# Windowed attention with sinks and a gated feed-forward block on one core: an early gate unit, scores in threes, and groups 2 and 3 turned by the crossbar

## The chip, the cores and the metric

The kernel runs on one core of a Trainium2 chip. The metric is device time in microseconds for one launch. The engines named here are TensorE (PE, with PEld for its weight loads), VectorE (DVE), ScalarE (ACT), GpSimd (POOL) and SyncE (SP). POOL and SP, and in places ACT, also issue the transfers (DMAs), which all run on the same sixteen DMA engines.

## What is computed

Attention over 4 batches, 8 heads, 768 positions and head size 64, in which a query sees the last 128 positions and the first 4 ("sinks"), followed by a gated feed-forward block on all 3072 tokens:

```python
keep = is_sink | in_window            # pos < 4, or 0 <= q - k < 128
a = softmax(where(keep, q @ k.T / 8, -1e9))
x = (a @ v) as [3072 tokens, 512]
g = x @ w_gate                        # 512 x 1536
out = (g * sigmoid(g) * (x @ w_val)) @ w_out   # 1536 x 512
```

## The kernel before, in words

Tokens are handled in twelve groups of 256, three to a batch. Heads go in four pairs. For a group the attention steps are:

- **Loads.** POOL loads keys and queries (`natp`, four buffers) and values, with a cast to bf16. `load4` puts four tokens of each head in a row (two DMAs, for groups below `NPE = 4`); `load1` puts one token with all its heads in a row (four DMAs, for the others). `load_gate` and `load_out` load the feed-forward weights in chunks. POOL's queue is in order, and each of its loads waits for the load issued eight before it.
- **Turning keys and queries.** Scores need them with the head size on the partitions. For groups 0 to 3 TensorE does it (`step_T`: 64 small matmuls into PSUM, then copies by ACT and DVE). For groups 4 to 11 the crossbar does it (`cross_T`: two transposing DMAs on SP's queue, for the two halves of 128 tokens). `C(g)` is `cross_T(g)` and then the load of group g+4.
- **Scores.** `step_S(g, p2)` computes two head pairs into four PSUM banks; ACT takes exponentials, DVE multiplies by the mask. `step_K(g)` does the scores against the four sinks for all heads, `step_ks` first collects their keys, and `build_vsb` builds on POOL the table of sink values.
- **Values.** `step_PV(g, j, hh)` multiplies by the values for one half of the tokens and four heads; DVE (and for half of group 1 ACT) normalises into `xn`.
- **Turning the output.** For groups below `NXPE = 5` by TensorE (`step_X`), for others by a transposing DMA on SP's queue.

The feed-forward block works on eight blocks of tokens (`SIZES`: three of 256, four of 512, one of 256); block 3 is groups 3 and 4. A `gate` unit projects 512 columns twice (`pg` for the gate, `pv` for the value), with a tanh on ACT between and two DVE operations that make `ht`; `down` multiplies 128 tokens of `ht` by `w_out` and stores the result by SP.

The order is written out by hand. `weave` walks through a list of units (gates, then downs, of one or more blocks), and runs the attention steps of each unit's slot in the middle of it: in a gate between `pg` and `pv`, in a down spread over its twelve matmuls. DVE operations of attention steps are put in the list `later` and issued after the gate's own product, by `flush`. PSUM has eight banks, given out in turn to every product.

At the start TensorE does groups 0 and 1 with little feed-forward work to mix in. Line numbers below are those of the profile.

Of the kernel before, what the change touches and what calls it, by code (L numbers as in the profile page):

```python
# [8 lines left out]
FP32 = mybir.dt.float32  # L9
# [6 lines left out]
def kernel(  # L16
# [12 lines left out]
    nc = tc.nc  # L29
# [13 lines left out]
    SIZES = [256, 256, 256, 512, 512, 512, 512, 256]  # L43
    assert sum(SIZES) == NTOK and NG == 12 and S == 768
    OFF = [sum(SIZES[:i]) for i in range(len(SIZES))]
    NPE = 4
    NXPE = 5
    VS = 72
    FCH = [2, 2, 2, 2, 4]
    assert sum(FCH) == DFC  # L50
# [4 lines left out]
    def pool(name, bufs, psum=False):  # L55
        if psum:
            return ctx.enter_context(
                tc.tile_pool(name=name, bufs=bufs, space=bass.MemoryType.PSUM))
        return ctx.enter_context(tc.tile_pool(name=name, bufs=bufs))
# [2 lines left out]
    wpool = pool("wpool", 1)  # L62
    natp = pool("natp", 4)
    vpool = pool("vpool", 1)
    kqtp = pool("kqtp", 3)
    crossp = pool("crossp", 4)
    epool = pool("epool", 2)
    espool = pool("espool", 2)
# [11 lines left out]
    def bank(shape, dtype, name):  # L80
        return psum.tile(shape, dtype, tag="b", name=name)
# [121 lines left out]
    for ks in kss:  # L203
# [8 lines left out]
        out=dh, in_=dh, compare_op=ALU.is_ge, fill=0.0, base=NS - 1,  # L212
        pattern=[[32, NP2], [NS, 2]], channel_multiplier=-1)
    load_v(1)
    build_vsb(0)
    for i in range(1, 5):
        load_gate(i)

    def build_masks():

# [87 lines left out]
    def step_ks(b):  # L308

        dst = kss[b].rearrange("q (a m) -> q a m", m=KS)  # L310
        for h in range(2):
# [2 lines left out]
                out=dst[r, :, h * NS:(h + 1) * NS],  # L314
                in_=kTs[b * GC][r, :, 0:NS] if b * GC < NPE
                else cross[b * GC][r, 0, 0, :, 0:NS])
    def step_S(g, p2):

        b, c = divmod(g, GC)
        if p2 == 0:  # L320
            e_t[g] = epool.tile([P, H, 512], BF16, tag="e", name="e")

        parts = [(2 * c, 0, 2, P), (2 * c + 1, 1, 1, 3 * P)]
        if c > 0:
            parts.insert(0, (2 * c - 1, 0, 1, 0))
        lo = 0 if c > 0 else P
        pss = [bank([P, 512], FP32, "s") for _ in range(4)]
        for pp in range(2):
            p = 2 * p2 + pp
            for t, j, n, col in parts:  # L330
                for h in range(2):
                    r = slice(h * D, (h + 1) * D)
                    nc.tensor.matmul(  # L333
                        pss[2 * pp + h][:, col:col + n * P], keys(b, t, r, p),
                        queries(g, r, p, j, n), start=True, stop=True)
        m = (mask if c > 0 else mask0).rearrange("q (o a) x -> q o (a x)", o=1)
        for pp in range(2):
            h0 = 4 * p2 + 2 * pp
            for h in range(2):
                nc.scalar.activation(  # L340
                    e_t[g][:, h0 + h, lo:512], pss[2 * pp + h][:, lo:512],
                    AF.Exp, scale=scale)

            def dve(e=e_t[g][:, h0:h0 + 2, lo:512]):
                nc.vector.tensor_tensor(  # L345
                    e, e, m[:, :, lo:512].broadcast_to([P, 2, 512 - lo]), op=ALU.mult)
            later.append(dve)

    def step_K(g):
        b, c = divmod(g, GC)  # L350
        if c == 0:
            return
        ps = bank([P, 256], FP32, "pk")
        for p in range(NP2):

            nc.tensor.matmul(
                ps[KS * p:KS * (p + 1)], kss[b][:, p * KS:(p + 1) * KS],
                queries(g, slice(0, P), p, 0, 2), start=True, stop=True)
        es_t[g] = espool.tile([P, 256], BF16, tag="es", name="es")
        nc.scalar.activation(es_t[g], ps, AF.Exp, scale=scale)  # L360

    def step_PV(g, j, hh, act=False):
        b, c = divmod(g, GC)
# [61 lines left out]

    hts = {}

    def gate(tb, f, attn):

        n = SIZES[tb]  # L430
        two = 512 // n
        if tb not in hts:
            t = hpool.tile([P, DFC * 512], BF16, tag="ht", name="ht")
            hts[tb] = dense(t, DFC, n)
            if tb == 0:
                hts[1] = t[:, DFC * n:2 * DFC * n].rearrange("p (c n) -> p c n", c=DFC)
        x = xTs[tb]

        def project(ws, name):
            ps = bank([P, 512], FP32, name)  # L440
            for i in range(two):
                fi, fo = FOF[f + i]
                for c in range(DMC):
                    nc.tensor.matmul(  # L444
                        ps[:, i * n:(i + 1) * n], ws[fi][:, c, fo * P:(fo + 1) * P],
                        x[:, 0:n // P, c], start=(c == 0), stop=(c == DMC - 1))
            return ps

        pg = project(wgs, "pg")
        th = tpool.tile([P, 512], FP32, tag="th", name="th")  # L450
        nc.scalar.activation(th, pg, AF.Tanh, scale=0.5)  # L451
        for a in attn:
            a()
        pv = project(wvs, "pv")

        u = upool.tile([P, 512], BF16, tag="u", name="u")
        nc.vector.scalar_tensor_tensor(u, th, 1.0, pg, op0=ALU.add, op1=ALU.mult)  # L457
        nc.vector.tensor_tensor(  # L458
            hts[tb][:, f:f + two].rearrange("p a n -> p (a n)"), u, pv, op=ALU.mult)
        flush()  # L460

    def last_down(tb, ts):

# [57 lines left out]
        return [A(step_T, g, 0), last]  # L521

    def Ss(g):
        return [A(step_S, g, p2) for p2 in range(2)]

    def PVs(g):

# [4 lines left out]

    def K(g):
        return A(step_K, g)

    def weave(us, slots):
        assert all(i < len(us) for i in slots)
# [31 lines left out]
    first_T(0)  # L569
    build_masks()  # L570
    first_T(1)
    step_S(0, 0)
    warm(1)
    step_S(0, 1)
    warm(2)
    pro(*[lambda: None] * 3)
    step_PV(0, 0, 0)
# [8 lines left out]
    step_T(1, 1, q_late=True)  # L586
    flush()
    step_ks(0)
    step_S(1, 0)
    load4(2)  # L590
    load_v(2)
    for i in range(4):
        load_out(i)
# [2 lines left out]
    for g in (3, 4):  # L596
# [2 lines left out]


    g0, g1, g2 = gates(0), gates(1), gates(2)
    us = [g0[0], (alone, 0, 0), *g0[1:3], *g1[0:3], g0[3], *g1[3:6], *g0[4:6],
          *downs(0), *g2, *downs(1), *downs(2)]
    p1 = [A(step_PV, 1, j, hh, j == 1) for hh in range(2) for j in range(2)]
    weave(us, slots(
        (0, [flush, A(step_S, 1, 1), K(1), A(next_load, 1)]), (1, p1[:2]), (2, p1[2:] + [flush]),
        (3, [A(step_X, 1, 0), A(step_X, 1, 1, True), flush]),
        (9, T(2)), ((10, 11), Ss(2)), (11, [K(2)]),
        (12, PVs(2)[:2] + [flush]), (13, PVs(2)[2:] + [flush]), (13, C(4)),
        (14, [A(step_X, 2, 0), A(step_X, 2, 1, True), flush]),  # L610
        (15, T(3)), ((16, 17), Ss(3)), (17, sinks(1)), ((18, 18, 19, 19), PVs(3)),
        (18, C(5)), ((20, 21), Ss(4)), (21, Xs(3) + [K(4)]),
        ((22, 22, 23, 23), PVs(4)), (24, Xs(4))))

    def pair(ga, gb, sh=0):
        s = sh
        return [((s, s + 2), Ss(ga)), (s + 2, [K(ga)]),
                ((s + 4, s + 5, s + 6, s + 7), PVs(ga)),
                ((s + 6, s + 8), Ss(gb)), (s + 8, [K(gb)]),
                ((11, 11, 12, 12) if s else (10, 11, 12, 13), PVs(gb))]  # L620

    weave(gates(3) + downs(3), slots(
        *pair(5, 6, 2), (2, C(6)), (10, C(7))))
    weave(gates(4) + downs(4), slots((0, sinks(2)), *pair(7, 8), (3, C(8)), (10, C(9)), (14, C(10))))
    weave(gates(5) + downs(5), slots((0, sinks(3)), *pair(9, 10), (10, C(11))))
    weave(gates(6) + gates(7) + downs(6) + downs(7), slots(
        ((0, 2), Ss(11)), (2, [K(11)]), ((4, 5, 6, 7), PVs(11))))


# [33 lines left out]
```

## Time and profile before

| | |
|---|---|
| median of 13 runs | 246.49 us (245.25 to 247.63) |
| the profiled execution: time, span | 247.39 us, 245.7 us |
| TensorE busy, instructions | 235.3 us (96%), 2081 |
| VectorE, ScalarE, GpSimd busy | 65%, 45%, 29% |
| transfers on POOL's queue (q0) | 68832 packets, 13.90 MB |
| transfers on SP's and ACT's queue (q1) | 28416 packets, 12.49 MB |
| pg and pv of all gates (L444) | 74.7 and 74.9 us busy |
| down (L490) | 63.8 us busy |

The span runs from the first instruction to the last; the device time is 1.7 us longer. In the slices of the page each digit is a busy share in tenths of one fortieth of the span (6.14 us). A row of PE's timeline gives start, duration, line, operation and, in brackets, the idle time ahead of it and who ended it. Rows of DMA queues give packets, megabytes as they land, and the time of the packets as a share of sixteen engines; since several packets can be under way at once, the share passes 100%.

### The profile page before, as it was taken

What the parts mean: (1) busy time and instruction counts of PE and PEld (TensorE: products, weight loads), DVE (VectorE), ACT (ScalarE), POOL (GpSimd) and SP (SyncE); (2) the same over time, 40 slices, a digit from 0 to 9 for tenths busy, and PEclk for the clock granted to TensorE, in tenths of its full rate; (3) what the DMA queues carried; (4) which work ended last, traced back from release to release, by engine and by line L of the source; (5) the groups of instructions that cost most, each with busy time, mean ns of one, the idle gap of its engine ahead of it and who ended that gap; (6) DMA issues with size and microseconds to landing.
All of it is one profiled execution on the core that took longest, in us unless ns stands there. A gap on an engine that the chain in (4) does not pass through costs nothing.

```text
span 245.7 us, 5202 instructions
## 1 busy us (share of the span) xinstructions
PE 235.3 (96%) x2081; PEld 136.8 (56%) x2081; DVE 160.4 (65%) x338; ACT 111.8 (45%) x221; POOL 71.2 (29%) x92
## 2 busy tenths in 40 slices
PE   7796999999999999999999999999999999999994
PEld 2475888757855445554445454445454445488443
DVE  2786688937994388891398980398980389877100
ACT  2657436627481365442665612656512662232111
POOL 8796395784279505307100000000000000000000
PEclk9978899999999999999999999999999999999999
DMA  7999999999999995959960244900334200200132
GB/s 138 169 169 179 204 190 204 164 148 172 162 154 175 204 176 53 113 106 110 236 98 1 48 82 129 173 0 1 64 67 131 85 0 3 43 0 3 48 123 87
DMA packets 97704, 27.11 MB, mean 110 GB/s; under 512 B 83728, under 2 KB 94736, under 8 KB 97680
## 3 DMA queue, kind: packets, MB, share of 16 engines
q0 software_dynamic: 68832, 13.90, 67.6%
q1 hardware_dynamic: 28416, 12.49, 24.0%
q10 hardware_dynamic: 432, 0.39, 0.5%
q8 instruction: 16, 0.26, 0.4%
q14 instruction: 8, 0.07, 0.1%
HBM read 28.34 MB, written 6.29 MB: 141 GB/s over the span
## 4 chain that ended last, share of the span: by engine, by line
PE 83%; ACT 6%; DVE 5%; DMA 3%; issue 2%; POOL 0%; DVEq 0%; POOLq 0%; ACTq 0%
PE pd L490 24%; PE pv L444 24%; PE pg L444 22%; PE o L380 6%; ACT e L340 4%; PE s L333 3%; PE pt L269 2%; DMA kq<-in_k_dram 2%; DVE ht L458 1%; DVE u L457 1%; DVE e L345 1%; PE px L416 1%; ACT th L451 1%; DMA out_dram<-ot 1%; DVE xn L392 1%
## 5 line engine op out<-in xcount | busy, mean ns | idle before, releaser
L444 PE MATMUL pv<-xT,wv 128*128 128x256 bf16 (+1 forms) x384 | 74.9, 328 | 1.1 <-DVE ht L458 1.1
L444 PE MATMUL pg<-xT,wg 128*128 128x256 bf16 (+1 forms) x384 | 74.7, 327 | 0.0
L451 ACT ACTIVATE th<-pg 128x512 f32<-128x512 f32 x72 | 43.5, 604 | 61.3 <-PE pg L444 60.8
L457 DVE SCALAR_TENSOR_TENSOR u<-th,pg 128x512 bf16<-128x512 f32 x72 | 49.2, 683 | 30.2 <-ACT th L451 29.7
L490 PE MATMUL pd<-wo,ht 128*128 128x512 bf16 x276 | 63.8, 379 | 0.0
L458 DVE TENSOR_TENSOR ht<-u,pv 128x512 bf16<-128x512 bf16 x72 | 49.5, 688 | 10.7 <-PE pv L444 3.3
L444 PEld LDWEIGHTS <-wg 128*128 128x128 bf16 x384 | 37.5, 98 | 25.5 <-issue 0.2
L444 PEld LDWEIGHTS <-wv 128*128 128x128 bf16 x384 | 34.8, 98 | 21.4 <-issue 3.1
L340 ACT ACTIVATE e<-s 128x512 bf16<-128x512 f32 (+1 forms) x96 | 46.1, 580 | 0.4 <-PE s L333 0.3
L490 PEld LDWEIGHTS <-ht 128*128 128x128 bf16 x276 | 25.7, 97 | 27.6 <-issue 0.2
L494 ACT ACTIVATE ot<-pd 128x512 f32<-128x512 f32 x23 | 13.7, 597 | 53.8 <-PE pd L490 53.8
L345 DVE TENSOR_TENSOR e<-e,mask 128x1024 bf16<-128x1024 bf16 (+1 forms) x48 | 28.9, 641 | 1.4 <-ACT e L340 1.3
L123 POOL DMA_DIRECT2D va<-in_v_dram x24 | 21.3, 892 | 6.3 <-DMA kq<-in_k_dram 3.4
L107 POOL DMA_DIRECT2D kq<-in_k_dram x16 | 14.2, 885 | 26.5 <-DMA kqT<-kq 23.1
L380 PEld LDWEIGHTS <-e 128*128 128x128 bf16 x352 | 17.1, 100 | 7.4 <-DVE e L345 2.1
L392 DVE TENSOR_TENSOR xn<-o,rcp 128x256 bf16<-128x256 f32 x46 | 19.5, 424 | 1.6
L380 PE MATMUL o<-va,e 128*128 128x65 bf16 x352 | 18.8, 197 | 1.4 <-DVE e L345 1.4
L107 POOL DMA_DIRECT2D kq<-in_q_dram x16 | 14.2, 885 | 6.0 <-DMA va<-in_v_dram 2.5
L385 DVE RECIPROCAL rcp<-o 128x4 f32<-128x4 f32 x48 | 8.5, 177 | 10.1 <-PE o L380 10.1
L380 PE MATMUL o<-vsb,es 128*128 128x260 bf16 x32 | 9.1, 283 | 2.5 <-ACT es L360 2.5
L274 DVE CAST qT<-pt 128x512 bf16<-128x512 f32 x7 | 4.6, 687 | 8.5 <-PE pt L269 8.5
L475 DVE TENSOR_SCALAR ot<-pd 128x256 f32<-128x256 f32 x1 | 0.4, 424 | 14.4 <-DMA out_dram<-ot 14.4
(61 smaller groups left out, 109.7 us busy)
## 6 DMA issues: line engine op xcount, KB each, us to landing
out_dram<-ot SPq DMA_DIRECT2D x23, 256.0 KB
va<-in_v_dram POOLq DMA_DIRECT2D x24, 128.0 KB, 7.4
kq<-in_k_dram POOLq DMA_DIRECT2D x18, 128.0 KB, 7.2
kq<-in_q_dram POOLq DMA_DIRECT2D x16, 128.0 KB, 7.6
wo<-in_moe_w_out_dram POOLq DMA_DIRECT2D x4, 384.0 KB, 12.7
wg<-in_moe_w_gate_dram POOLq DMA_DIRECT2D x4, 256.0 KB, 6.8
wv<-in_moe_w_val_dram POOLq DMA_DIRECT2D x4, 256.0 KB, 7.4
kq<-in_k_dram POOLq DMA_DIRECT2D x3, 256.0 KB, 9.9
```

What stands on the lines that cost most here:

```text
L107: nc.gpsimd.dma_start(x[:, j, i].rearrange("p (h d) -> p h d", d=D), src[b, :, t0:t0 + P].rearrange("h m d -> m h d"))
L123: nc.gpsimd.dma_start(va[:, j, :, 0:D], v[b, :, t0:t0 + P].rearrange("h m d -> m h d"))
L340: nc.scalar.activation(e_t[g][:, h0 + h, lo:512], pss[2 * pp + h][:, lo:512], AF.Exp, scale=scale)
L345: nc.vector.tensor_tensor(e, e, m[:, :, lo:512].broadcast_to([P, 2, 512 - lo]), op=ALU.mult)
L380: nc.tensor.matmul(o, l, r, start=(i == 0), stop=(i == len(mms) - 1), skip_group_check=True)
L392: nc.vector.tensor_tensor(xns[g, j][:, 256 * hh:256 * (hh + 1)].rearrange("p (h d) -> p h d", h=4), po[:, :, 0:D], rcp.broadcast_to([P, 4, ...
L444: nc.tensor.matmul(ps[:, i * n:(i + 1) * n], ws[fi][:, c, fo * P:(fo + 1) * P], x[:, 0:n // P, c], start=(c == 0), stop=(c == DMC - 1))
L451: nc.scalar.activation(th, pg, AF.Tanh, scale=0.5)
L457: nc.vector.scalar_tensor_tensor(u, th, 1.0, pg, op0=ALU.add, op1=ALU.mult)
L458: nc.vector.tensor_tensor(hts[tb][:, f:f + two].rearrange("p a n -> p (a n)"), u, pv, op=ALU.mult)
L490: nc.tensor.matmul(po, hts[tb][:, f, ts * P:(ts + 1) * P], wos[f // n][:, f % n], start=(f == 0), stop=(f == DFC - 1))
L494: nc.scalar.activation(ot, po, AF.Copy, scale=0.5)
```

## The change

What the new version does:

- `NPE` falls from 4 to 2 and `NXPE` from 5 to 3: groups 2 and 3 are loaded by `load1` and turned by `cross_T` on SP's queue, and the outputs of groups 3 and 4 are turned by transposing DMAs. The steps `T(2)`, `T(3)`, `Xs(3)`, `Xs(4)` are gone; `C(2)` and `C(3)` are placed in units 2 and 8. The buffers `kqtp` are two instead of three.
- `step_S` takes a list of (group, pair); groups 3 to 10 are done two groups together, three pairs at a time (`S3`), into six banks, in three visits in place of four.
- `step_K` does two groups of a batch in one step, with one exponential, for groups 4 and 5, 7 and 8, 10 and 11.
- At the start the second gate unit of block 0 stands ahead of group 1's values (`held_gate`); its DVE product is held back until after their normalisation (`first_PVs`), and the four value products of group 1 run together.
- The loads of gate weights 1 to 4 are issued before the first sink table is built.
- Block 1's downs come ahead of block 2's gates, and the slots are placed anew. `C(8)` and the later ones stand earlier.

```diff
-    NPE = 4
-    NXPE = 5
+    NPE = 2
+    NXPE = 3
...
-    kqtp = pool("kqtp", 3)
+    kqtp = pool("kqtp", 2)
...
     load_v(1)
+    load_gate(1)
+    for i in range(2, 5):
+        load_gate(i)
     build_vsb(0)
-    for i in range(1, 5):
-        load_gate(i)
...
-    def step_S(g, p2):
+    def step_S(*pairs):
+        runs = []
+        for g, p in pairs:
+            b, c = divmod(g, GC)
...
+            pss = [bank([P, 512], FP32, "s") for _ in range(2)]
+            runs.append((g, p, 0 if c > 0 else P, pss))
...
     def step_K(g):
         b, c = divmod(g, GC)
-        if c == 0:
-            return
-        ps = bank([P, 256], FP32, "pk")
-        for p in range(NP2):
+        n = 1 if g < GC else GC - c
+        ps = bank([P, n, 256], FP32, "pk")
+        for i in range(n):
+            for p in range(NP2):
...
+        es = espool.tile([P, 2, 256], BF16, tag="es", name="es")
+        nc.scalar.activation(es[:, 0:n], ps, AF.Exp, scale=scale)
...
-    def gate(tb, f, attn):
+    def gate(tb, f, attn, hold=False):
...
+        if hold:
+            later.append(product)
+        else:
+            product()
+            flush()
...
+    def S3(ga, gb):
+        hs = [(ga, p) for p in range(NP2)] + [(gb, p) for p in range(NP2)]
+        return [A(step_S, *hs[i:i + 3]) for i in range(0, 2 * NP2, 3)]
...
-    load4(2)
+    load1(2)
...
-    us = [g0[0], (alone, 0, 0), *g0[1:3], *g1[0:3], g0[3], *g1[3:6], *g0[4:6],
-          *downs(0), *g2, *downs(1), *downs(2)]
+    def first_PVs():
+        held = later[:]
+        later.clear()
+        for j, hh in ((0, 0), (1, 0), (0, 1), (1, 1)):
+            step_PV(1, j, hh, j == 1)
+        flush()
+        later.extend(held)
+
+    us = [g0[0], (held_gate, 0, 2), (alone, 0, 0), g0[2], *g1[0:3], g0[3], *g1[3:6],
+          *g0[4:6], *downs(0), *downs(1), *g2, *downs(2)]
     weave(us, slots(
-        (0, [flush, A(step_S, 1, 1), K(1), A(next_load, 1)]), (1, p1[:2]), (2, p1[2:] + [flush]),
-        (3, [A(step_X, 1, 0), A(step_X, 1, 1, True), flush]),
-        (9, T(2)), ((10, 11), Ss(2)), (11, [K(2)]),
-        (12, PVs(2)[:2] + [flush]), (13, PVs(2)[2:] + [flush]), (13, C(4)),
-        (14, [A(step_X, 2, 0), A(step_X, 2, 1, True), flush]),
-        (15, T(3)), ((16, 17), Ss(3)), (17, sinks(1)), ((18, 18, 19, 19), PVs(3)),
-        (18, C(5)), ((20, 21), Ss(4)), (21, Xs(3) + [K(4)]),
-        ((22, 22, 23, 23), PVs(4)), (24, Xs(4))))
+        (0, [flush, A(step_S, (1, 2), (1, 3)), K(1), A(next_load, 1)]), (2, [first_PVs]),
+        (2, C(2)), (3, [A(step_X, 1, 0), A(step_X, 1, 1, True), flush]), (8, C(3)),
+        ((11, 12), Ss(2)), (11, [K(2)]), (13, PVs(2)[:2] + [flush]),
+        (14, PVs(2)[2:] + [flush]), (14, C(4)),
+        (15, [A(step_X, 2, 0), A(step_X, 2, 1, True), flush]),
+        (15, C(5)), ((16, 18, 20), S3(3, 4)), (17, sinks(1)), ((17, 17, 19, 19), PVs(3)),
+        (19, [K(4)]), ((21, 21, 22, 22), PVs(4))))
...
     def pair(ga, gb, sh=0):
         s = sh
-        return [((s, s + 2), Ss(ga)), (s + 2, [K(ga)]),
-                ((s + 4, s + 5, s + 6, s + 7), PVs(ga)),
-                ((s + 6, s + 8), Ss(gb)), (s + 8, [K(gb)]),
+        return [((s, s + 3, s + 6), S3(ga, gb)), ((s + 2, s + 4, s + 5, s + 7), PVs(ga)),
                 ((11, 11, 12, 12) if s else (10, 11, 12, 13), PVs(gb))]
...
-        *pair(5, 6, 2), (2, C(6)), (10, C(7))))
-    weave(gates(4) + downs(4), slots((0, sinks(2)), *pair(7, 8), (3, C(8)), (10, C(9)), (14, C(10))))
-    weave(gates(5) + downs(5), slots((0, sinks(3)), *pair(9, 10), (10, C(11))))
+        *pair(5, 6, 2), (2, C(6)), (10, C(7)), (14, C(8))))
+    weave(gates(4) + downs(4), slots(
+        (0, sinks(2)), *pair(7, 8), (1, [K(7)]), (5, C(9)), (10, C(10)), (14, C(11))))
+    weave(gates(5) + downs(5), slots(
+        (0, sinks(3)), *pair(9, 10), (5, [K(10)])))
     weave(gates(6) + gates(7) + downs(6) + downs(7), slots(
-        ((0, 2), Ss(11)), (2, [K(11)]), ((4, 5, 6, 7), PVs(11))))
+        ((0, 2), Ss(11)), ((4, 5, 6, 7), PVs(11))))
```

## The prediction

> **What bounds the kernel now.** I first read the page: busy shares, slices and the chain that ended last.
>
> ```profile
> PE 235.3 (96%) x2081; PEld 136.8 (56%) x2081; DVE 160.4 (65%) x338; ACT 111.8 (45%) x221; POOL 71.2 (29%) x92
> ...
> PE   7796999999999999999999999999999999999994
> ...
> PEclk9978899999999999999999999999999999999999
> DMA  7999999999999995959960244900334200200132
> ...
> PE 83%; ACT 6%; DVE 5%; DMA 3%; issue 2%; POOL 0%; DVEq 0%; POOLq 0%; ACTq 0%
> ```
>
> TensorE (PE) is busy almost everywhere, and its order is fixed, so removing its work helps wherever nothing else is late. Two things stand out: a hole with a lower clock in slices 2 to 5, and a DMA row at 9 for the first 15 slices (92 us). The second decides this change.
>
> The hole, in the busy times of two stretches (PE second after the width, then PEld, DVE, ACT, POOL, clock) and in PE's timeline:
>
> ```profile
> 19.30:22.70 3.40, 1.29 (x24) 1.08 (x23) 3.24 (x9) 2.17 (x5) 2.43 (x4) 0.99 1.40 183
> 22.70:26.00 3.30, 3.30 (x30) 2.56 (x28) 1.48 (x6) 2.19 (x9) 1.83 (x3) 0.50 1.36 202
> ```
>
> ```profile
> 18.37 1.05 PE L444 MATMUL pv<-xT,wv 128*128 128x256 bf16 x8
> 21.52 0.28 PE L380 MATMUL o<-vsb,es 128*128 128x260 bf16 x1 [2.11 <-ACT es L360]
> ...
> 37.25 1.04 PE L444 MATMUL pg<-xT,wg 128*128 128x256 bf16 x8
> 38.22 1.09 PE L269 MATMUL pt<-ident,kq 64*64 64x64 bf16 x64
> 39.24 1.05 PE L444 MATMUL pv<-xT,wv 128*128 128x256 bf16 x8
> ```
>
> PE waits 2.11 us for group 1's sink exponentials, then runs 3.3 us at half clock. The last three lines price a turn by TensorE: 39.24 - 37.25 less the 0.87 that a pg takes alone = 1.12 us.
>
> DMA: the queue rows (packets, MB, share) of four stretches, in this order: 38 to 41 us (w_out alone), 47 to 53 (loads by heads, 128 B packets, alone), 62 to 68 (such loads beside a crossbar pair), 107 to 111 (crossbar alone).
>
> ```profile
> q0 software_dynamic: 624, 0.62, 124.0%
> ...
> q0 software_dynamic: 7199, 0.91, 243.3%
> ...
> q0 software_dynamic: 2438, 0.31, 84.6%
> q1 hardware_dynamic: 2055, 0.57, 82.2%
> ...
> q1 hardware_dynamic: 2634, 0.65, 85.9%
> ```
>
> Per us: 208, 1200, then 406 beside 342, and about 800 where the crossbar runs by itself. Side by side the two queues move nearly equal packet counts, and the loads drop to a third. Finally SyncE (SP) around group 4's pair:
>
> ```profile
> 49.30 1.33 SPq L303 DMA_TRANSPOSE kqT<-kq  x1
> 51.18 3.84 SPq L303 DMA_TRANSPOSE kqT<-kq  x1
> ```
>
> SP stands from 7.1 to 49.3 until group 4's rows have landed. The first crossbar packets appear only at 53.5, the last at 60: 10.7 us for a pair among loads. Alone, at 107.11, POOL's wait for the pair ends at 112.1: 5 us. Before, that slowness hides, since group 4's scores come at 67.1.
>
> [...] here 2.1 us idle in a stretch of 3.4 was enough for 3.3 us at 0.50, so a stall costs some 1.7 us more than itself.
>
> **The change part by part.** The sum is against the profiled execution (247.39 us, span 245.7), 0.9 above the median of the runs; I apply the difference to the median.
>
> Front. Two projections (1.75 us at full clock) move into the hole, from 19.24 to 21.0; their weights landed at about 18.2 and 19.5 (issues 13.45 and 14.26, shortest landings 4.7 and 5.2), and are now issued before the sink table. Values follow at 21.5, when es is done (ACT's order there is unchanged but for a 0.6 us tanh after es), four products of 0.37 to 23.0, at full clock. VectorE normalises its share of the halves (22.1 to 23.6, as now 0.18 + 0.42 each; ScalarE's two halves of 0.93 follow one another and end at 24.7), then does the held product (0.68 + 0.69, to 25.0). Block 0's third unit cannot put its second turn of group 1's values before 24.7 nor its pv before 25.0, so block 1's first unit starts at about 25.95 instead of 28.52: -2.6. Some 0.5 and 0.65 us of idling stay. The later sink table (1.44 us on POOL, behind eight issues of 0.78 from 10.5) is done near 19.2, before 21.5: nothing, with 2.3 us of cover.
>
> Turns removed. Groups 2 and 3: 2 x 1.12 = -2.2. Groups 3 and 4's outputs: each two times four px at 0.22 to 0.23 (70.66 to 70.89 and 71.53 to 71.76 for group 3), 2 x 0.45 = -0.9. Their evictions leave ACT and DVE, at 45% and 65%: nothing on the path.
>
> Scores three pairs at a time: for groups 3 to 10 sixteen visits become twelve; a visit costs 0.10 to change tile shape (pg to s 0.97 against 0.87): -0.4, 0.1 of it in the first 80 us. Sink scores joined in twos: same matmuls, a few ACT fixed costs saved off the path; but group 5's move up to unit 19. Six of eight PSUM banks per visit makes PE meet late exponentials: before, with four, PE lost 0.2 to 0.45 us at three such places. I take +0.3 over the four pairs, bounds -0.2 and +3.
>
> Without new waits that is -2.6 - 2.2 - 0.9 - 0.4 + 0.3 = -5.8.
>
> New waits. Groups 2 and 3 are loaded by heads: 4096 packets of 128 B (3.4 us at 1200) in place of 1024 of 512 B (2.6 us): +0.8 us each on the load queue; POOL issues 4 x 0.88 for 2 x 0.72, hidden, as up to eight loads stand in the queue. Two crossbar pairs (2048 packets each) now fall in the saturated stretch. Each takes at least 2.6 us from the loads (2048 / 800) and at most 4.0 (6 us at 406 instead of 1200, in 62 to 68).
>
> First wait: scores of group 2 (unit 11). Unit 11's pg starts at 25.95 + 7 x 1.746 = 38.2, so PE asks at 39.1. The last gate weights land at 30.6 (POOL's wait), less the 0.5 us of a gap at 18 us that earlier issues fill; behind them, at 0.85 per load, group 2's two halves land at about 32 and 33.7, and the pair then shares the engines with v and w_out, whose packets go at 208 alone and at 165 or fewer beside crossbar packets. 1300 packets beside v and 750 at 165: 42 at the earliest; with the 4 us start seen at 49.30: 46. A stall of 3 to 7 us.
>
> Second wait: group 5's sink scores (K(4), unit 19). Unit by unit from 39.1 (gate 1.75; visit 0.65 for two pairs, 41.64 - 40.12 - 0.87, and 0.92 for three; down 2.59; two sink-and-value products 0.74) PE asks at 62.5. Before, group 5's last rows landed at 60.4 (POOL's wait for them) and were wanted at 87. Now: 60.4 + 2 x 0.8 + two pairs (5.1 to 8.0) - 0.5 (that gap) = 66.6 to 69.5. Then its own pair: 3.5 at the least (second half of a lone pair), 8.1 as measured for it before (issue 60.10, last packet 68.2). Landed: 70 to 77.6; I take 74, and keep 68 and 78 for errors in landing lag. The wait at unit 11 is swallowed: with 5 us and 1.7 of slow clock PE would reach unit 19 at 69. So +11.5 at unit 19, +1.7 for the clock after it. Behind it on PE is everything; on SP the stores and group 3's output transposes stand behind group 5's pair, with four output buffers, so no stall before block 2's downs.
>
> Third: group 4's output transposes are issued in unit 22, 6 us before block 3 needs them; 10.7 us for a pair twice as large among loads, 4 us for two alone: 0 to 2, I take +0.5.
>
> Sum: -5.8 + 11.5 + 1.7 + 0.5 = +7.9: 255.3 for such an execution, 254.4 for the median.
>
> **The rivals.** (1) The crossbar keeps up: PE runs on, 246.5 - 5.8 = 240.7. For it: crossbar packets alone go at 800 per us, and group 2's rows land 5 us ahead of need. Against: the DMA row at 9. It decides where group 5's pair lands before 62.5 + 5.8 = 68.3; my lowest bound is 68, so even a break-even needs every bound at its kind end. (2) A small stall: pair landed at 68 to 70.5, no clock loss: 246 to 249. (3) The banks: if each of eight further visits costs 1 us, +8 from there with the DMA in time, -6.1 + 8: 248.4; against it, in the stretch 118 to 192 PE lost under 0.7 us in all to VectorE. (4) Block 0's second unit finds its weights late: the front gains 1 instead of 2.6; swallowed by the stall.
>
> **How the numbers follow.** Both waits, 249 to 259.5: 0.61. Small stall or banks, 245.7 to 249: 0.16. Crossbar keeps up, 239 to 245.7: 0.17. Worse than 259.5: 0.06. The range 245.7 to 259.5 leaves these last two out; 249 to 259.5 is the likeliest case's own. About 0.3% (0.7 us) is what a measurement tells from no change: faster 0.18, same 0.05, slower 0.77.
>
> **What would show it.** PE waiting for DMA kqT at the score line near 39 us and at the sink-score line near 70; half clock after each; crossbar packets at equal counts with w_out's near 36 to 43. No hole at 19 to 21.5, pg of block 1 near 26. Wrong if those waits are absent or under 3 us together, if w_out does not slow the crossbar, or if PE's idling sits at DVE and ACT in block 3 and later.

## The result, and the profile after

The changed kernel takes 272.37 us (median of 11 runs, 270.25 to 273.75) against 246.42 us before (48 runs): 1.1048 times the time [1.1026, 1.1071], 26 us slower. The direction was forecast, the size was not: the forecast was 254.4 us and its range ended at 259.5. The profiled execution took 272.23 us with a span of 270.4 (before: 247.39 and 245.7).

The page of the changed kernel: busy shares, the slices of PE, its clock and the DMA engines (6.76 us each), and the chain that ended last.

```profile
PE 238.7 (88%) x1937; PEld 135.7 (50%) x1937; DVE 156.2 (58%) x330; ACT 109.0 (40%) x214; POOL 75.2 (28%) x96
...
PE   8789960999849919999994999999999999999994
...
PEclk9999997599977977999997999999999999999999
DMA  9999999999999998932699213371030320100122
...
PE 56%; DMA 29%; POOL 4%; SPq 4%; DVE 3%; ACT 2%; issue 1%; POOLq 0%; DVEq 0%; ACTq 0%
```

PE issues 144 instructions fewer and yet is busy 3.4 us longer: there are stretches at half clock (0.50 to 0.54, below). The hole at 19 to 26 us is gone. In its place are four others, at slices 6 and 7, 12, 15 and 22 (counted from 1), each with a low clock in or after it. DMA's share of the chain went from 3% to 29%. What PE waited for, in the view of waits (total us, times, longest):

```profile
PE s L334 <- DMA kqT<-kq: 9.9, 3, 6.4
PE pk L358 <- DMA kqT<-kq: 7.2, 2, 3.8
PE pg L448 <- DMA xT<-xn: 5.8, 1, 5.8
```

22.9 us, and all of it for crossbar transposes. PE's timeline places them (start, duration, operation, and in brackets the wait ahead of it):

```profile
18.82 1.05 PE L448 MATMUL pg<-xT,wg 128*128 128x256 bf16 x8
20.13 1.05 PE L448 MATMUL pv<-xT,wv 128*128 128x256 bf16 x8 [0.26 <-DMA wv<-in_moe_w_val_dram]
...
25.10 1.03 PE L448 MATMUL pg<-xT,wg 128*128 128x256 bf16 x8
...
44.74 0.29 PE L334 MATMUL s<-kqT,kT 64*128 64x128 bf16 x2 [6.38 <-DMA kqT<-kq]
47.88 0.50 PE L334 MATMUL s<-kqT 64*128 64x256 bf16 x4 [2.85 <-DMA kqT<-kq]
...
71.64 0.56 PE L334 MATMUL s<-kqT 64*128 64x256 bf16 x10 [0.68 <-DMA kqT<-kq]
78.97 0.41 PE L358 MATMUL pk<-kqT,ks 128*32 128x256 bf16 x4 [3.84 <-DMA kqT<-kq]
101.06 1.86 PE L448 MATMUL pg<-xT,wg 128*128 128x512 bf16 x4 [5.79 <-DMA xT<-xn]
146.39 0.40 PE L358 MATMUL pk<-kqT,ks 128*32 128x256 bf16 x4 [3.33 <-DMA kqT<-kq]
```

The first three lines are the new front: the second unit stands in the old hole and block 1 begins at 25.10 (before: 28.52). Then come the four stalls: group 2's scores (in two parts, one for each half of its tokens), `K(4)` with group 5's share of it, block 3's first projection, and `K(7)` with group 8's share. The 0.68 us at 71.64 are for the second half of group 4's pair. The clock after each of the four, from the busy times of four stretches (clock third from the end):

```profile
47.90:51.30 3.40, 3.40 (x25) 2.21 (x25) 0.30 (x1) 2.34 (x5) 3.17 (x4) 0.50 2.99 149
79.00:83.00 4.00, 4.00 (x24) 2.49 (x26) 1.70 (x5) 0.65 (x2) 2.83 (x4) 0.50 2.15 191
101.00:104.50 3.50, 3.44 (x9) 1.27 (x10) 0.69 (x1) 0.60 (x1) 0.00 (x0) 0.50 1.40 220
146.40:149.60 3.20, 3.20 (x12) 1.20 (x13) 0.69 (x1) 0.60 (x1) 0.00 (x0) 0.54 1.27 185
```

Half of 14.1 us, as an estimate from these widths and clocks: some 7 us that the waits cost beside themselves. SP's timeline shows how the transposes were issued (`out_dram` lines are stores, `xT` lines turn outputs):

```profile
58.67 0.38 SPq L507 DMA_DIRECT2D out_dram<-ot  x1
59.16 5.94 SPq L304 DMA_TRANSPOSE kqT<-kq  x2
65.19 0.54 SPq L507 DMA_DIRECT2D out_dram<-ot  x1
65.84 2.96 SPq L304 DMA_TRANSPOSE kqT<-kq  x1
68.91 4.03 SPq L304 DMA_TRANSPOSE kqT<-kq  x1
...
92.49 2.50 SPq L402 DMA_TRANSPOSE xT<-xn  x2
...
135.11 4.56 SPq L304 DMA_TRANSPOSE kqT<-kq  x2
```

Group 4's pair stands behind the store of block 0's first down, which needs PE, which is waiting for group 2. So the first stall also delays the issue of group 4's pair (49.30 before, 59.16 now), and group 5's pair (65.84 and 68.91, one row for each half) stands behind that one and another store.

By stretches of the span, from the first `pg` of each block:

| | before | after | difference |
|---|---|---|---|
| start to block 3 | 82.80 | 101.06 | +18.3 |
| block 3 | 35.85 | 37.91 | +2.1 |
| block 4 | 37.24 | 41.91 | +4.7 |
| block 5 | 36.42 | 36.42 | 0.0 |
| the rest | 53.4 | 53.1 | -0.3 |
| span | 245.7 | 270.4 | +24.7 |

### The profile page after: what moved, and what is told of

Its sections match the earlier page's. It is cut to its first block, busy times and chain, and to the rows that moved or that the text cites. A ratio compares the mean times of both kernels' runs of the same rounds, so it can differ in the third digit from the quotient of the medians.

```text
span 270.4 us, 4926 instructions
## 1 busy us (share of the span) xinstructions
PE 238.7 (88%) x1937; PEld 135.7 (50%) x1937; DVE 156.2 (58%) x330; ACT 109.0 (40%) x214; POOL 75.2 (28%) x96
## 4 chain that ended last, share of the span: by engine, by line
PE 56%; DMA 29%; POOL 4%; SPq 4%; DVE 3%; ACT 2%; issue 1%; POOLq 0%; DVEq 0%; ACTq 0%
PE pv L448 19%; PE pg L448 17%; PE pd L501 14%; DMA kqT<-kq 13%; DMA xT<-xn 5%; DMA kq<-in_q_dram 4%; DMA wv<-in_moe_w_val_dram 4%; SPq L304 3%; PE o L384 3%; PE s L334 2%; DMA kq<-in_k_dram 1%; POOL va L123 1%; POOL wg L132 1%; ACT e L340 1%; DVE ht L463 1%
## 5 line engine op out<-in xcount | busy, mean ns | idle before, releaser
L448 PE MATMUL pg<-xT,wg 128*128 128x256 bf16 (+1 forms) x384 | 77.5, 337 | 5.9 <-DMA xT<-xn 5.8
L448 PE MATMUL pv<-xT,wv 128*128 128x256 bf16 (+1 forms) x384 | 78.2, 339 | 0.4 <-DMA wv<-in_moe_w_val_dram 0.3
L501 PE MATMUL pd<-wo,ht 128*128 128x512 bf16 x276 | 62.6, 379 | 0.0
L448 PEld LDWEIGHTS <-wg 128*128 128x128 bf16 x384 | 38.6, 101 | 34.0 <-issue 8.9
L448 PEld LDWEIGHTS <-wv 128*128 128x128 bf16 x384 | 35.6, 101 | 22.7 <-issue 4.9
L107 POOL DMA_DIRECT2D kq<-in_k_dram x20 | 17.8, 889 | 40.2 <-DMA kqT<-kq 32.6
L107 POOL DMA_DIRECT2D kq<-in_q_dram x20 | 17.7, 885 | 5.9 <-DMA kq<-in_q_dram 3.3
L384 PE MATMUL o<-va,e 128*128 128x65 bf16 x352 | 18.0, 193 | 1.2 <-DVE e L345 1.2
L334 PE MATMUL s<-kqT 64*128 64x256 bf16 (+1 forms) x208 | 12.7, 253 | 4.0 <-DMA kqT<-kq 3.5
L334 PEld LDWEIGHTS <-kqT 64*128 64x128 bf16 x208 | 7.7, 99 | 10.7 <-issue 10.4
## 6 DMA issues: line engine op xcount, KB each, us to landing
wo<-in_moe_w_out_dram POOLq DMA_DIRECT2D x4, 384.0 KB, 10.2
```

The lines of the kernel that those rows point to most:

```text
L107: nc.gpsimd.dma_start(x[:, j, i].rearrange("p (h d) -> p h d", d=D), src[b, :, t0:t0 + P].rearrange("h m d -> m h d"))
L334: nc.tensor.matmul(pss[h][:, col:col + n * P], keys(b, t, r, p), queries(g, r, p, j, n), start=True, stop=True)
L384: nc.tensor.matmul(o, l, r, start=(i == 0), stop=(i == len(mms) - 1), skip_group_check=True)
L448: nc.tensor.matmul(ps[:, i * n:(i + 1) * n], ws[fi][:, c, fo * P:(fo + 1) * P], x[:, 0:n // P, c], start=(c == 0), stop=(c == DMC - 1))
L501: nc.tensor.matmul(po, hts[tb][:, f, ts * P:(ts + 1) * P], wos[f // n][:, f % n], start=(f == 0), stop=(f == DFC - 1))
```

## The experiments

My theory after the result: four parts of the change (turns, joined sink scores, output transposes, three-pair visits) each cost by themselves, because a crossbar transpose among loads lands some 9 to 15 us after its issue and the new order asks sooner. The rivals: one stall (group 2's) delays everything behind it, or the traffic of two more pairs does the harm wherever they are asked for. "Before" in the ratios is the kernel before, run on the same chip.

### The front alone

```diff
-    build_vsb(0)
     for i in range(1, 5):
         load_gate(i)
+    build_vsb(0)
...
-    us = [g0[0], (alone, 0, 0), *g0[1:3], *g1[0:3], g0[3], *g1[3:6], *g0[4:6],
+    us = [g0[0], (held_gate, 0, 2), (alone, 0, 0), g0[2], *g1[0:3], g0[3], *g1[3:6], *g0[4:6],
```

`held_gate` and `first_PVs` are those of the change; the rest is the kernel before.

> The kernel before with the front part alone: second gate unit ahead of group 1's values, product held, first sink table built after the gate weights. Theory (the front is a gain, the crossbar turns of groups 2 and 3 are the loss): block 1's first pg moves from 28.5 to about 25.5, nothing later is touched, time 243.0 to 244.0. Rival (the front is not covered, its weights or its late product hold up block 1): 246 or more.

Measured: 244.45 us, ratio 0.9926 [0.9903, 0.9949]. In its timeline of PE:

```profile
19.25 1.04 PE L444 MATMUL pg<-xT,wg 128*128 128x256 bf16 x8
20.49 1.05 PE L444 MATMUL pv<-xT,wv 128*128 128x256 bf16 x8 [0.20 <-DMA wv<-in_moe_w_val_dram]
21.52 0.28 PE L380 MATMUL o<-vsb,es 128*128 128x260 bf16 x1
...
26.46 1.03 PE L444 MATMUL pg<-xT,wg 128*128 128x256 bf16 x8
```

Block 1 begins at 26.46, 2.1 us earlier than before. This part gains about 2 us by itself. That is a little under the forecast's 2.6, and the time lies just above the 243.0 to 244.0 expected here; two output turns of group 1 now wait 0.15 and 0.18 us for ScalarE's halves, which is a part of the difference.

### Groups 2 and 3 by crossbar, alone

```diff
-    NPE = 4
+    NPE = 2
...
-    load4(2)
+    load1(2)
...
-        (9, T(2)), ((10, 11), Ss(2)), (11, [K(2)]),
+        (2, C(2)), (8, C(3)), ((10, 11), Ss(2)), (11, [K(2)]),
...
-        (15, T(3)), ((16, 17), Ss(3)), (17, sinks(1)), ((18, 18, 19, 19), PVs(3)),
+        ((16, 17), Ss(3)), (17, sinks(1)), ((18, 18, 19, 19), PVs(3)),
```

> The kernel before with one part alone: groups 2 and 3 loaded by heads and turned by the crossbar; scores by two pairs, sink scores of each group by itself, outputs of groups 3 and 4 by TensorE, no front part. Theory: group 2's scores, asked at about 40, wait for the pair until 46 to 48.5, 1.7 us more go to the half clock, later waits are gone because group 5 is asked late; minus 2.2 for the two turns: 251 to 254. Rival (three-pair visits, joined sink scores or output transposes are to blame, not the pairs of groups 2 and 3): 244, with no wait over 1 us at group 2's scores.

Measured: 254.25 us, ratio 1.0333 [1.0286, 1.0381], some 8 us slower, just above the 251 to 254 expected. PE's timeline:

```profile
44.82 0.29 PE L333 MATMUL s<-kqT,kT 64*128 64x128 bf16 x2 [5.42 <-DMA kqT<-kq]
47.55 0.51 PE L333 MATMUL s<-kqT 64*128 64x256 bf16 x4 [2.44 <-DMA kqT<-kq]
```

7.9 us of waits and 1.7 of slow clock (the `pv` and `pg` after the scores took 1.89 and 1.91 us, for 1.05 and 1.04 later on), less the 2.2 of the turns: 7.4, near enough. No later wait for a DMA is left in this kernel. So with the demand for groups 4 and 5 where it was, this stall does not bring the others about.

### The traffic without the demand

The kernel before, with two pairs for groups 2 and 3 into a spare tile that nobody reads; TensorE turns the groups as before.

```diff
+    def dead_T(g):
+        t = crossp.tile([P, 2, 2, NP2, P], BF16, tag="dead", name="dead")
+        for j in range(2):
+            nc.sync.dma_start(
+                t[:, j].rearrange("q i a m -> q (i a) m"),
+                nat[g][:, 4 * j:4 * j + 4].rearrange("p h x -> p (h x)"), transpose=True)
...
-        (9, T(2)), ((10, 11), Ss(2)), (11, [K(2)]),
+        (2, [A(dead_T, 2)]), (8, [A(dead_T, 3)]), (9, T(2)), ((10, 11), Ss(2)), (11, [K(2)]),
```

> The kernel before with two added crossbar pairs whose results nobody reads: the rows of groups 2 and 3 are transposed into a spare tile, while TensorE turns them as before. It measures the transfers without a demand. Theory: group 5's last rows land at 67 to 70 instead of 60.4, group 4's scores (asked at 67) wait 0 to 3 us, time 246.5 to 250. Rival (the traffic by itself makes most of the loss of the turns alone, 7.8 us): 251 to 255.

Measured: 248.83 us, ratio 1.0089 [1.0053, 1.0125]. One wait is new in PE's timeline:

```profile
68.18 0.34 PE L341 MATMUL s<-kqT 64*128 64x256 bf16 x4 [1.83 <-DMA kqT<-kq]
```

It is that of group 4's scores, late by the two pairs ahead of it. The traffic of the pairs costs 2.2 us by the ratio (1.3 to 3.1), somewhat over a quarter of what the second experiment lost. The rest is the demand and the loads by heads, which this run leaves out together: no run tells these two apart.

### Groups 2 and 3 back, all else of the change kept

```diff
-    NPE = 2
+    NPE = 4
...
-        (2, C(2)), (3, [A(step_X, 1, 0), A(step_X, 1, 1, True), flush]), (8, C(3)),
+        (3, [A(step_X, 1, 0), A(step_X, 1, 1, True), flush]), (9, T(2)),
...
-        (14, PVs(2)[2:] + [flush]), (14, C(4)),
+        (14, PVs(2)[2:] + [flush]), (14, T(3) + C(4)),
```

(With `load4(2)` and three `kqtp` buffers, as before.)

> The changed kernel with groups 2 and 3 loaded by fours and turned by TensorE again, all else kept. Theory in its narrow form (only the turns of groups 2 and 3 cost): 241 to 244. Theory in its wide form (every early demand on a crossbar transfer costs, turns of groups 2 and 3 being the largest): no wait at group 2's scores; group 5's sink scores asked at about 65 and its pair landed at 69 as before, 4 us and 1.7 of half clock; output transposes of group 4 2 to 6 late; group 8's sink scores 3 late: 253 to 259. Rival (the banks): still over 265 with waits on exponentials.

Measured: 264.13 us, ratio 1.0676 [1.06, 1.0751]. PE's timeline of the profiled execution (265.3 us; the four runs took 260.93 to 265.3):

```profile
70.70 0.40 PE L358 MATMUL pk<-kqT,ks 128*32 128x256 bf16 x4 [4.35 <-DMA kqT<-kq]
...
93.03 1.87 PE L448 MATMUL pg<-xT,wg 128*128 128x512 bf16 x4 [6.18 <-DMA xT<-xn]
...
138.90 0.41 PE L358 MATMUL pk<-kqT,ks 128*32 128x256 bf16 x4 [4.37 <-DMA kqT<-kq]
```

The theory of one stall falls. Without group 2's stall the other three stand, each as long or longer, and two thirds of the loss remain. The time is above both expectations: I had expected the waits and again priced them too low.

### Sink scores group by group

```diff
-        n = 1 if g < GC else GC - c
+        n = 1
...
-        *pair(5, 6, 2), (2, C(6)), (10, C(7)), (14, C(8))))
+        *pair(5, 6, 2), (3, [K(5)]), (2, C(6)), (10, C(7)), (14, C(8))))
...
-        (0, sinks(2)), *pair(7, 8), (1, [K(7)]), (5, C(9)), (10, C(10)), (14, C(11))))
+        (0, sinks(2)), *pair(7, 8), (1, [K(7)]), (6, [K(8)]), (5, C(9)), (10, C(10)), (14, C(11))))
```

(`K(11)` likewise has a step of its own.) The same exponentials are computed, in three steps more.

> The changed kernel with the sink scores of groups 5, 8 and 11 asked with their own group instead of one group earlier. Theory: the waits at 75 to 79 and 143 to 146 go, with their half clocks: about 5.5 and 5 us, some of the first handed on to the wait for group 4's output transposes: 261 to 266. Rival (these waits only take up time that would be lost at the next crossbar transfer): 270 or more.

Measured: 262.22 us, ratio 1.064 [1.0598, 1.0682], 10.2 us less than the changed kernel. The waits of PE that are left for DMAs:

```profile
PE s L334 <- DMA kqT<-kq: 8.6, 3, 5.8
PE pg L448 <- DMA xT<-xn: 5.8, 1, 5.8
```

Both waits at `pk` are gone, with the slow clock after them (the `pv` behind each takes 1.05 and 1.02 us, for 1.89 at both in the changed kernel), and nothing takes their place. Joining the steps saved three small ACT operations (in the changed kernel an exponential for two groups takes 0.60 us, for one 0.45) and asked for groups 5 and 8 several units earlier.

### The outputs of groups 3 and 4 by TensorE

```diff
-    NXPE = 3
+    NXPE = 5
...
-        (19, [K(4)]), ((21, 21, 22, 22), PVs(4))))
+        (19, [K(4)]), (20, Xs(3)), ((21, 21, 22, 22), PVs(4)), (24, Xs(4))))
```

> The changed kernel with the outputs of groups 3 and 4 turned by TensorE again. Theory: the wait of 5.8 us ahead of block 3 goes with the half clock after it (1.9), 0.9 comes back on TensorE: 265 to 267. Rival (block 3's start is bound by other transfers): 270 or more.

Measured: 265.86 us, ratio 1.0792 [1.075, 1.0834], 6.5 us less than the changed kernel: the wait of 5.79 us and its clock are gone (block 3's first `pg` takes 1.03 us, for 1.86), and TensorE has the sixteen output turns back (40 `px` matmuls for 24), 0.9 us by the forecast's price. The two waits at `pk` grew to 4.29 and 4.47.

### Both of these

The edits of the last two together.

> The changed kernel with two things taken back together: sink scores of groups 5, 8 and 11 with their own group (alone: 262.2 for 272.4) and outputs of groups 3 and 4 by TensorE (alone: 265.9). Theory (each wait adds its own time and half clock): 272.4 - 10.2 - 6.5 = 255.7, so 254.5 to 257. Rival (one wait hides behind another): 259 or more.

Measured: 257.35 us, ratio 1.0458 [1.0406, 1.051], 15.0 us less than the changed kernel where the single edits sum to 16.7. That is just above the 254.5 to 257 of the theory, and under the rival's 259. PE's timeline:

```profile
44.45 0.29 PE L334 MATMUL s<-kqT,kT 64*128 64x128 bf16 x2 [4.81 <-DMA kqT<-kq]
47.39 0.50 PE L334 MATMUL s<-kqT 64*128 64x256 bf16 x4 [2.65 <-DMA kqT<-kq]
...
102.39 0.51 PE L334 MATMUL s<-kqT 64*128 64x256 bf16 x8 [2.63 <-DMA kqT<-kq]
136.97 0.56 PE L334 MATMUL s<-kqT 64*128 64x256 bf16 x10 [1.82 <-DMA kqT<-kq]
```

With PE earlier, a new demand shows: the second visit of three pairs already takes two pairs of group 6 (and later of group 8). The changed kernel has no wait at these two places; its earlier stalls probably gave these transposes the time.

### Is group 5's late pair the cause, or group 2's?

Group 2's loads are moved ahead of gate weights 3 and 4, so that its pair lands in time.

```diff
-    for i in range(2, 5):
+    load_gate(2)
+    load1(2)
+    for i in range(3, 5):
         load_gate(i)
...
-    load1(2)
```

> The changed kernel with group 2's keys and queries loaded ahead of gate weights 3 and 4, so that the pair is done ahead of w_out. Theory: group 2's scores, asked at 38.3, no longer wait more than 1 us; but the same packets still stand ahead of group 5's rows, so group 5's sink scores are reached near 66 and stand until 76 to 79: time 269 to 273 in spite of 9 us less waiting and 1.7 us less half clock earlier on. Rival (the wait at group 2's scores is a cost of its own): 261 to 264.

Measured: 275.59 us, ratio 1.1195 [1.1143, 1.1248]. PE's timeline:

```profile
24.76 0.27 PE L386 MATMUL o<-vsb,es 128*128 128x260 bf16 x1 [3.73 <-POOL vsb L188]
62.85 0.67 PE L336 MATMUL s<-kqT 64*128 64x256 bf16 x12 [4.49 <-DMA kqT<-kq]
...
81.34 0.40 PE L360 MATMUL pk<-kqT,ks 128*32 128x256 bf16 x4 [7.27 <-DMA kqT<-kq]
```

Group 2's scores no longer wait, and nothing is gained by it: PE waits at later demands instead, 4.49 us at group 3's scores and 7.27 at group 5's sink scores, until 81.34. The forecast's "swallowed" fits: the end of the stall at group 5 sets the time. That end did not stay where it was, though: SP got group 5's last rows at 72.8, where it had them by 68.9 in the changed kernel, and no run shows why. The edit also put group 2's four load issues ahead of the sink table on POOL, and PE waited 3.73 us for that table at the front. That no theory had foreseen; it may be why the time lies above the expected 269 to 273.

### Shorter packets beside the crossbar

Each load of `w_out` is cut in two by columns, so that its packets are half as long; twice as many issues.

```diff
-        nc.gpsimd.dma_start(
-            t, moe_w_out[i * n * P:(i + 1) * n * P].rearrange("(c p) f -> p c f", p=P))
+        for s in (slice(0, DM // 2), slice(DM // 2, DM)):
+            nc.gpsimd.dma_start(
+                t[:, :, s],
+                moe_w_out[i * n * P:(i + 1) * n * P, s].rearrange("(c p) f -> p c f", p=P))
```

> The changed kernel with each w_out load cut into two by columns: the same bytes in packets half as long. Theory (engines alternate between queues packet by packet, so long packets on one queue slow the crossbar on the other): group 2's pair goes at 240 to 280 packets per us beside w_out instead of 160, lands 2 to 4 us earlier, and the wait at group 2's scores shrinks by as much. But group 5's sink scores still stand until about 79, so the whole time moves by under 1.5 us: 271 to 273. Rival (each wait adds to the total): 268 to 270. Rival on the rate (crossbar packets are slow by themselves, or share by bytes): 160 per us as before.

Queue rows of the changed kernel from 38 to 40 us (packets, MB, share), beside whole `w_out` packets:

```profile
q0 software_dynamic: 317, 0.31, 91.8%
q1 hardware_dynamic: 316, 0.08, 30.1%
```

and of this kernel from 43 to 45, beside half packets (the profiled execution took 278.86 us; the four runs, 274.0 to 278.86):

```profile
q0 software_dynamic: 493, 0.24, 87.0%
q1 hardware_dynamic: 502, 0.13, 47.1%
```

Per us 158 crossbar packets became 251, with one packet of the other queue to each in both cases: in these stretches the length of the other queue's packets, 0.98 KB and 0.49 KB, set the crossbar's pace. Yet the kernel took 275.33 us, ratio 1.1161 [1.1104, 1.1218], above the 271 to 273 expected. Group 2's scores resumed at 47.04 in place of 47.88, and `K(4)` at 81.34 in place of 78.97. The effect of packet length is shown for this pair of lengths; as a remedy it failed. One difference is on record: the four further issues of `w_out` on POOL put group 3's loads, and those behind them, later (first issue at 40.23 for 36.53). Whether that is the cause was not tested.

### The visits of three pairs

What is left of the change when groups 2 and 3 are turned by TensorE, sink scores are separate, and group 4's output is turned by TensorE: the front, the visits of three pairs, group 3's output by crossbar and the placement of the slots.

> All early demands on the crossbar taken back, the rest of the change kept: groups 2 and 3 by TensorE, sink scores of groups 5, 8 and 11 with their own group, group 4's output by TensorE, group 3's by crossbar; early gate unit and three-pair visits as changed. Theory: no wait on a DMA over 1 us, time 243 to 244.3, the front's gain plus 0.4 for group 3's output and about 0.4 for the visits. Rival (three-pair visits cost in banks): 246 or more.

Measured: 248.83 us, ratio 1.0103 [1.006, 1.0145]. PE's timeline:

```profile
78.05 1.47 PE L501 MATMUL pd<-wo,ht 128*128 128x512 bf16 x6 [1.20 <-DVE ht L463]
94.86 0.51 PE L334 MATMUL s<-kqT 64*128 64x256 bf16 x8 [1.78 <-DMA kqT<-kq]
128.50 0.56 PE L334 MATMUL s<-kqT 64*128 64x256 bf16 x10 [0.88 <-DMA kqT<-kq]
```

The time is in the rival's range, but the waits are mostly of another kind: 3.0 us for crossbar pairs in three places, and 1.2 for VectorE. The visits are not free: the middle one asks for the second group's transposes two or three units sooner. To take that away I set the block order as before and issued `C(6)` to `C(10)` earlier:

```diff
-           *g0[4:6], *downs(0), *downs(1), *g2, *downs(2)]
+           *g0[4:6], *downs(0), *g2, *downs(1), *downs(2)]
...
-        *pair(5, 6, 2), (3, [K(5)]), (2, C(6)), (10, C(7)), (14, C(8))))
+        *pair(5, 6, 2), (3, [K(5)]), (2, C(7)), (9, C(8))))
```

(with `C(4)` in unit 15, `C(5)` in 18 and `C(6)` in 20 of the first stretch, and `C(9)` and `C(10)` in units 0 and 8 of block 4's. Block order and earlier issue were changed together, so neither has a price of its own.)

> The kernel of run e8_pe_own (front, three-pair visits, groups 2 and 3 and the output of group 4 by TensorE, own sink scores) with the crossbar turns of groups 6 to 11 issued earlier and block 2's gates ahead of block 1's downs as before. Theory (what was left in e8_pe_own were waits of 0.4, 1.8 and 0.9 for crossbar pairs that three-pair visits ask earlier, and 1.2 for VectorE where no down stood between): waits for DMA under 0.5 in all, 243.2 to 244.5. Rival (the visits cost in banks or VectorE): 246 or more.

Measured: 253.29 us, ratio 1.0276 [1.0243, 1.0309], worse. PE and SP, one fence each:

```profile
63.08 0.29 PE L334 MATMUL s<-kqT,kT 64*128 64x128 bf16 x2 [2.85 <-DMA kqT<-kq]
66.39 0.50 PE L334 MATMUL s<-kqT 64*128 64x256 bf16 x4 [3.02 <-DMA kqT<-kq]
```

```profile
53.12 12.99 SPq L304 DMA_TRANSPOSE kqT<-kq  x4
```

`C(4)` in unit 15 had come behind stores on SP and was issued at 53.12; group 4's scores paid for it. With `C(4)` alone put back in unit 13:

> The kernel of run r10_early_c with group 4's crossbar pair issued in unit 13 again, ahead of block 0's two stores on SP, as in the kernel before; nothing else differs. Theory (r10_early_c lost 5.9 us and half clocks only because that pair stood behind two stores; three-pair visits cost nothing by themselves once no transfer is asked early): no wait on a crossbar pair over 0.5, 243.0 to 244.3, level with r9_front_x3 (243.84) or up to 0.6 under it. Rival (three-pair visits cost by themselves, through banks or VectorE): 245 or more, with waits on exponentials or ht.

Measured: 246.93 us (22 runs), ratio 1.0027 [1.0005, 1.0049]. No wait for the crossbar is left, and two units of `C(4)` were worth 6.4 us. Still it does not reach the 243 to 244.3 that I expected; it lies in the range of the rival, that the visits cost by themselves.

### The front, with group 3's output by crossbar

The first experiment's kernel plus one edit: no `Xs(3)`, group 3's output turned on SP's queue.

```diff
-        if hh == 1 and g >= NXPE:
+        if hh == 1 and (g == 3 or g >= NXPE):
...
-          (18, C(5)), ((20, 21), Ss(4)), (21, Xs(3) + [K(4)]),
+          (18, C(5)), ((20, 21), Ss(4)), (21, [K(4)]),
```

> The kernel before with the front part, and with the output of group 3 alone turned by the crossbar: a transfer asked some 14 us after its issue. Theory (a crossbar transfer is free where its demand is far off): 243.7 to 244.3, 0.45 under the front alone (244.45). Rival (any added crossbar transfer in the saturated stretch holds up block 3): 245 or more.

Measured: 243.84 us (243.36 to 245.6), ratio 0.9908 [0.9875, 0.9941]. PE waits nowhere for a transpose. It is the fastest of all, faster than both kernels; its lead over the front alone, 0.6 us, is within what the runs can tell.

The last kernel of the previous section differs from this one in the three-pair visits and the places of `C(6)`, the later transposes, sink scores and value products that go with them, and is 3.1 us slower in the medians. In the two profiled executions (246.19 and 243.70 us) 1.0 us of 2.5 lies ahead of block 1, where the first kernel ran at 0.50 and 0.51 of the clock from 12.6 to 19 us and the second at 1.00; 0.8 lies in blocks 1 and 2, and 0.7 in blocks 3 to 5. Busy times of the stretch from 60 to 70 us, first the kernel with three-pair visits, then the one without:

```profile
60.00:70.00 10.00, 8.98 (x103) 6.60 (x102) 9.05 (x24) 6.47 (x13) 4.15 (x6) 1.00 2.05 171
```

```profile
60.00:70.00 10.00, 9.53 (x105) 6.49 (x103) 9.27 (x23) 6.11 (x13) 3.50 (x4) 1.00 1.95 164
```

VectorE (third busy time) is nearly full in both, and PE is busy 0.5 us less with the visits: it waits there 0.84 us for VectorE, in three waits, and 0.41 in one without them. So 1.5 us (0.8 and 0.7) that can be the visits' cost are seen in the trace; the 1.0 ahead of block 1 is the clock of that execution. Why the medians differ by 3.1 stays open.

## Why the prediction was right and wrong

The mechanism that I named is there: a crossbar pair among loads lands after PE asks for it, and in the changed kernel the clock was 0.50 to 0.54 behind each of the four waits. The step that failed is the sum of the new waits. It gave one wait its full price, put +0.5 for group 4's output transposes, and nothing for group 8's sink scores. The runs showed three waits that add up: the one at group 5 ended 5.0 us later than I took, the one at the outputs cost 7.0 more, and the one at group 8 cost 4.8.

**The front, right.** -2.6 was forecast; block 1 began 3.4 us earlier, but 0.7 of that was there before the change's first new instruction (block 0's first `pg` at 15.91 for 16.61, the clock being 1.00 from 12.6 to 15.9 us, where the execution before had 0.51). That leaves -2.7; alone it gave -2.0.

**Turns and outputs, not net gains.** The 2.2 and 0.9 us fit the sums of the experiments with the turns alone and with the outputs back on TensorE. What was paid for them is larger: the two parts lose 7.8 and 6.5 us net.

**First wait, right place, mis-sized.** PE asked at 38.3 (forecast 39.1). The pair was complete at 47.9, where I had 42 to 46; beside `w_out` it moved one packet for one, 158 per us each (forecast: 165 or fewer, an estimate that agrees with the 208 and 800 of the forecast's stretches taken one packet for one). The wait was 9.2 us in two parts, not 3 to 7. In the changed kernel it is not a term of its own, as the experiment with group 2's early loads suggests; but it is what held back group 4's pair (issued at 49.45 where groups 2 and 3 are back on TensorE, at 59.16 here).

**Second wait, right place, mis-sized.** Group 5's last rows were there by 68.9, when SP issued the second half of its pair, inside the forecast's 66.6 to 69.5. Then I gave the pair 3.5 to 8.1 us, and took 74; from that issue it was 10.0 us until PE went on at 79.0, beyond my upper bound of 77.6 and the 78 kept for errors: +5.0. Of these, 3.0 come from taking the middle of my own bounds (68.9 and the measured 8.1 make 77.0), and 1.9 from a pair slower than that. In three kernels this half took 8.0 to 8.4 us (the kernel before, groups 2 and 3 back on TensorE, group 2's early loads). A likely reason for the 1.9 is SP's order, which the sum left out: group 4's pair stood behind a store that waits for the stalled PE, was still landing until PE took its second half at 71.64, and group 5's stands behind it in the same queue. That `C(4)` behind two stores cost 6.4 us, in the experiment with the earlier transposes, is the same effect elsewhere; here it was not tested.

**Third wait, wrong by ten times.** "0 to 2, I take +0.5" for group 4's output transposes. They were issued at 92.49, 2.8 us ahead of PE's need at 95.27 and not 6, and PE went on 8.6 us after their issue: from 92 to 96 us the crossbar's queue moved no packet, while loads went at 1226 per us. It measured 5.8, and 1.75 of slow clock (half of the 3.50 in the table of stretches), which I had given to no wait but the second: +7.0. Returning this part gave 6.5.

**Block 4, no step at all.** I priced the moved demand of `K(4)` on group 5 and left the same edit at `K(7)` on group 8 at nothing. Group 8's pair was issued at 135.11, was asked for at 143.06, and PE went on at 146.39, 11.3 us after the issue, beside group 11's loads: 3.3 of wait and 1.5 of slow clock, +4.8. The two waits at `pk` together are worth 10.2 us, the largest loss that a single edit gave back.

**Visits, wrong in sign.** -0.4 and +0.3 were forecast, the second with a bound of +3. In a kernel without waits for the crossbar they cost, with the places that go with them, between 1.5 and 3 us. The forecast priced tile shapes and banks, and left out that the middle visit asks for the second group sooner.

**A reading.** The 800 packets per us of a lone crossbar are not what the line shown gives: 2634 in four us are 659. Only the last of the four, 110 to 111 us, had 808; for some 0.5 us no packet moved.

Of these, the second wait, the third and block 4 sum to 5.0 + 7.0 + 4.8 = 16.8, which is what the span missed the forecast by (24.7 less 7.9). So close a fit is in part luck: the visits' share and the other differences must then cancel, and that was not shown. From the other side, the single experiments give -2.0 for the front, +7.8 for the turns, +10.2 for joined sink scores, +6.5 for the outputs and about +2.5 for the visits: 25.0 of the 26 measured, less the 1.7 by which two of them together fell short of their sum. Some of these were added to the kernel before and some taken from the changed one, so this sum is a rough one. The range failed because it let only one wait decide and gave a chance of 0.06 to all that lay beyond it; three waits were exposed to the same cause, and were not independent.

## What to carry to other kernels

Judge a crossbar transpose by the time from its issue to its first reader, in that stretch of the queues: 5 us alone, but 8.6 (group 4's outputs) to 15.4 (group 2's pair, 32.49 to 47.88) beside loads, and count what stands ahead of it on the issuing queue, stores that wait for the stalled engine included (behind one, group 4's pair was issued at 59.16 us instead of 49.45). Before two groups' steps are joined, look up when the second group's data land: the joined step has the demand time of the first. And a change that makes one transfer late must be followed through each later reader of the same queue, with the clock's price on each wait (1.5 to 2.0 us behind the changed kernel's four, by the table of stretches; none behind two waits named below), and not only to the first stall.

## What the runs showed of the hardware

While crossbar pairs were under way in the changed kernel, both queues came almost to rest for a while. The 0.125 us slices of 65 to 70 us show it (GB/s):

```profile
GB/s 163 158 159 161 156 157 160 162 156 159 161 156 159 154 150 278 142 148 149 144 144 101 80 24 7 10 9 9 9 50 133 162 159 157 156 162 162 157 155 157
```

About 0.8 us at 7 to 24 GB/s: from 68 to 68.5 us each queue moved 12 packets, and from 69 to 69.5 again 206 and 210. What stopped them is not shown. From 65 to 68 us the queues had moved 1150 and 1145 packets, 380 per us each; by these counts the loads lost about 290 packets in the 0.8 us (an estimate), and the crossbar moved hardly any in exchange.

A crossbar transpose by itself came near to the loads of `w_out` in bytes, at best: 808 packets of 256 B and 0.20 MB from 110 to 111 us of the kernel before, for `w_out`'s 0.21 MB per us. Beside loads of longer packets it did not: from 36 to 43 us of the changed kernel the crossbar moved 1034 packets and 0.26 MB, the loads 1156 packets and 1.11 MB.

Not every wait was followed by half clock. After single waits of 1.78 us (the first kernel with three-pair visits alone) and 2.63 us (sink scores apart and outputs by TensorE) the next 3.3 us ran at 1.00. After the changed kernel's waits it was at 0.50 to 0.54, and in the kernel before 3.3 us at 0.50 followed a wait of 2.11 us. So the length of a single wait does not tell by itself what it costs in clock. Nor was the clock the same at every start: the stretch from 12.6 to 15.9 us ran at 0.51 in the kernel before and at 1.00 in the changed one. What decides between the two clocks was not shown.
